# Halved weight splits, an earlier row eviction and moved logits and transposes in a fused attention and expert kernel

## The chip, the cores and the metric

The kernel runs on one core of one Trainium2 chip. A core has a matrix engine (TensorE, PE in the profile, with its weight loads as PEld), a vector engine (VectorE, DVE), a scalar engine (ScalarE, ACT), a general engine (GpSimd, POOL) and a queue engine that starts transfers (SyncE, SP). SBUF is the memory on the core, PSUM the memory with eight banks that TensorE writes its results to. The metric is the device time of one execution in microseconds (us).

## The reference

The input is an attention with a decaying state over 4 batches, 8 heads, 768 positions and a head dimension of 48, followed by a layer of 8 experts of which each token uses one:

```python
# attention, for each position t
cur = einsum('bhd,bhe->bhde', u * k_t, v_t)
y[t] = einsum('bhd,bhde->bhe', r_t, state + cur)
state = w_t[..., None] * state + einsum('bhd,bhe->bhde', k_t, v_t)
# experts, x is y as 3072 tokens x 384
logits = x @ w_gate + modality_bias[modality_id]
e = argmax(logits); gate = softmax(logits)[e]
out = gate * (relu(x @ w1[e]) @ w2[e])        # 384 -> 1024 -> 384
```

## The kernel before

**Attention.** The 3072 tokens are cut into NU = 24 units of 128, six for each batch. A loop runs i from -2 to 23 and calls `att_iter(i)`, which works on several units at once: the scans of unit a = i + 2, the products of unit m = i + 1, and the result of unit z = i. For unit a, VectorE makes two scans over the decays w (B, L251, and E, L254, 128x516 each). After that, R = r times E (L215) and, later, K = k times B (L221). POOL makes G = r times k behind the E scan (L256) and dV = v times dT (L262). For unit m, TensorE transposes K into bank pK (L283, not for the last unit of a batch), multiplies K with R into the banks pS0 and pS1 (L301), VectorE masks these into A (L303), and KT times v goes to pU (L310), from which ACT makes the next state SP. TensorE also sums G into a few columns of bank pT (`delta`, L233), which ACT copies to dT (L235). For unit z, TensorE adds a part from the state (L331) and a part from A (L337) into bank pY.

**What follows a unit's result.** One step later `x_rows` (L361) has VectorE evict pY plus dV into the rows of x, named xp. One more step later `x_cols` (L368) has TensorE transpose these rows into pT, ACT copies them to xT (L369), and `logits` (L374) multiplies xT with the gate's weights into bank pR. When 12 units are done, `route_a`, `route_b` (in `hook_b`) and `table` choose the experts on VectorE and make tables of blocks. They are put into the steps 14, 15 and 16 as hooks. From then on POOL scatters the rows of x to memory by expert, 2 or 3 units a step.

**Weights.** Products with weights are made of three: each weight is split into a rounded part wh (a cast on ACT, L206) and a rest wl (a subtraction, L207), and x and h likewise. Before the experts are known, w1 and w2 of a first expert e0 are loaded to raw[0] and raw[1] in quarters in steps 7 to 14 (L687). `w_split(0, f, 1, POOL)` splits one of the eight 128x384 parts f of w1 at a time, in the steps that `SPLITS = (10, 11, 12, 13, 14, 14, 16, 22)` names. In steps 3 to 6 the hooks `setup_a` to `setup_d` make a table of biases. They use a corner of raw[0] (bt2) for its second half.

**Experts.** Then come blocks of 256 tokens of one expert, for which `seq` gives the order. For block q, `blk_t` transposes the tokens into the banks pK and pU, ACT casts them to xh and VectorE subtracts to xo. `blk_up` makes the 1024 inner columns in four groups g of 18 matmuls each (L596), in the banks pS0, pS1 and pT in turn. ACT (hh, L601) and VectorE (hl, L602) empty each group. `blk_down` (L613) accumulates into pY and pX. In block 0 the last two units' transposes stand behind its groups 0 and 1, in pT, and their logits behind groups 2 and 3. The splits for the next block go along (`w_split(1, g)` on POOL and `w_split(0, g)` on VectorE).

**Order.** Every engine works in the order in which the program is written, and waits where data or a bank isn't ready. Tiles of one tag (`pt`) share a PSUM bank: pT holds the sums of `delta`, the transposes of `x_cols`, and a third of the groups of `blk_up`.

Of the kernel before, what the change touches and what calls it, by code (L numbers as in the profile page):

```python
# [9 lines left out]
F32 = mybir.dt.float32  # L10
# [4 lines left out]
ALU = mybir.AluOpType  # L15
# [37 lines left out]
def kernel(ctx: ExitStack, tc: tile.TileContext, rkw, vt, wf, cst, mid, wg, bias, w1, w2, out):  # L53
# [103 lines left out]
    m1 = cp.tile([P, 2, NU], F32, name="m1")  # L157
    bt2 = raw[0][:, 0, 0:NU * E].rearrange("p (a e) -> p a e", a=NU)
    bv = bb.rearrange("p (a e) -> p a e", a=2)
# [43 lines left out]

    def w_split(k, q, n=2, eng=None):
        sl = slice(n * q, n * q + n)
        nc.scalar.copy(out=wh[k][:, sl], in_=raw[k][:, sl])  # L206
        (eng or (nc.vector, nc.gpsimd)[k]).tensor_tensor(out=wl[k][:, sl], in0=raw[k][:, sl], in1=wh[k][:, sl].bitcast(F32), op=ALU.subtract)  # L207

# [14 lines left out]
    def first(n):  # L223
        return n % NCH == 0

    def ok(n):
        return 0 <= n < NU
# [9 lines left out]
    hooks = []  # L237
    done = iter(range(FC))

    SPLITS = (10, 11, 12, 13, 14, 14, 16, 22)  # L240

    def att_iter(i):
# [17 lines left out]
        if ok(z):  # L260
            dV = wt(z, "dV", [P, H, D], 2)
            nc.gpsimd.tensor_tensor(out=dV, in0=T["v", z].rearrange("p (a b) -> p a b", a=H),  # L262
                                    in1=T["dT", z].rearrange("p a b -> p (a b)")[:, :, None].to_broadcast([P, H, D]), op=ALU.mult)
        for _ in range(SPLITS.count(i)):
            w_split(0, next(done), 1, nc.gpsimd)
        if ok(z - 1):
            x_rows(z - 1)
# [6 lines left out]
        if ok(m):  # L274
# [5 lines left out]
            if not last:  # L280
# [6 lines left out]
                nc.scalar.copy(out=KT, in_=pK)  # L287
            if ok(z - 2):
                x_cols(z - 2, pT)
# [8 lines left out]
            for p in range(4):  # L298
                for hh in range(2):
                    q = slice(64 * hh, 64 * hh + 64)  # L300
                    nc.tensor.matmul(out=pS[hh][:, p], lhsT=K[q, p], rhs=R[q, p], start=True, stop=True)  # L301
            for hh in range(2):
                nc.vector.tensor_tensor(out=A[:, hh], in0=pS[hh], in1=mask[:, None, :].to_broadcast([P, 4, P]), op=ALU.mult)  # L303
            if ok(a):
                mk_k(a)
            if not last:
# [10 lines left out]
                for hh in range(2):  # L317
                    q = slice(64 * hh, 64 * hh + 64)
                    nc.scalar.copy(out=SPb[a % 3][q, :, hh], in_=SP[q])
        elif ok(z - 2):  # L320
            x_cols(z - 2, pt(m, "pT"))
        if ok(z - 2):
            logits(z - 2)
        if hooks:
            hooks.pop(0)()
        if ok(z):
            A, R, v, pY = T["A", z], T["R", z], T["v", z], pt(z, "pY")
            if not first(z):
                for p in range(4):
                    for q in (0, 64):  # L330
                        nc.tensor.matmul(out=pY[q:q + 64, 2 * p * D:2 * (p + 1) * D], lhsT=R[:, p, q:q + 64],  # L331
                                         rhs=SPb[z % 3][:, p].rearrange("p a b -> p (a b)"),
                                         start=(p == 0), stop=False, skip_group_check=True)
            for h in range(H):
                p, hh = divmod(h, 2)
                for q in (0, 64):
                    nc.tensor.matmul(out=pY[q:q + 64, h * D:(h + 1) * D], lhsT=A[:, hh, p, q:q + 64], rhs=v[:, h * D:(h + 1) * D],  # L337
                                     start=(first(z) and h == 0), stop=True, skip_group_check=True)
        if ok(m):
            delta(m)  # L340
# [235 lines left out]
    def blk_t(q):  # L576
# [10 lines left out]
        X["x", q] = (xh, xo)  # L587

    def blk_up(q, g):
        xh, xo = X["x", q]  # L590
        pp = pt(f"u{q}_{g}", ("pS0", "pS1", "pT")[(q * (FC // 2) + g) % 3] if isinstance(q, int) else f"pS{g % 2}", (P, 2, BT))
        for i in range(2):
# [90 lines left out]
    for i in range(-2, NU):  # L683
# [10 lines left out]
        if i == NU - 1:  # L694
            prep.close()
        att_iter(i)
        if i >= -1 and ok(i + 3):
            loadv(i + 3)
# [263 lines left out]
```

## Time and profile before

| what | us |
|---|---|
| median of 3 runs | 396.58 |
| the runs | 396.58, 398.23, 391.73 |
| the profiled execution | 392.17 |
| its span in the trace | 390.3 |
| first matmul of block 0, from the span's start | 154.5 |
| mean granted TensorE clock | 0.965 |

The trace is of one execution. In its views a row of the timeline gives the start, the duration, the engine, the line, the operation, output and inputs, and in brackets how long the engine was idle before it and what ended that. A duration in a timeline includes the latency of the instruction, so on one engine the next one can start a little before the end of the one before. Pieces of the chain of waits give start and length. A row of busy times by stretch gives start and end, the length, busy time and count for PE, PEld, DVE, ACT and POOL, then the granted clock as a share of full, the share of the DMA engines and their GB/s.

### The profile page before, as it was taken

The numbers are of one execution on the slowest core, as the hardware profiler recorded it, in microseconds if no ns is written. First come the engines' busy times: TensorE is split into PE (matmuls) and PEld (weight loads), VectorE is DVE, ScalarE is ACT, GpSimd is POOL, SyncE is SP. The second block draws the span as 40 slices with busy tenths as digits, with TensorE's granted clock in tenths as the row PEclk, the third lists the DMA queues.
The fourth block names the chain that finished last, engine by engine and source line by source line (L and its number), as shares of the span: only waits on it lengthen the run. The fifth ranks groups of instructions, "written<-read, shape, count | busy, mean of one in ns | idle before, by whom it ended". The sixth has DMA issues, their size and how long they took to land.

```text
span 390.3 us, 10893 instructions
## 1 busy us (share of the span) xinstructions
PE 360.5 (92%) x4280; PEld 343.7 (88%) x4280; DVE 246.7 (63%) x407; ACT 234.1 (60%) x480; POOL 226.3 (58%) x194
## 2 busy tenths in 40 slices
PE   5899899998877999999999999999999999999990
PEld 2688888887866988899999999999999999999990
DVE  6899999999998992675265936344261716651010
ACT  2476466668544662667468586777777675854330
POOL 6234643544878742576688895747466474736440
PEclk9589999999996999999999999999999999999996
DMA  7975779999467851001126543131313474166000
GB/s 153 216 159 135 169 187 215 226 235 211 110 162 193 210 187 51 1 3 42 60 103 223 154 171 117 48 122 39 104 43 101 127 260 135 45 208 196 9 28 21
DMA packets 18464, 50.52 MB, mean 129 GB/s; under 512 B 2917, under 2 KB 10635, under 8 KB 18404
## 3 DMA queue, kind: packets, MB, share of 16 engines
q1 hardware_dynamic: 15268, 40.28, 40.5%
q0 software_dynamic: 3136, 9.47, 6.8%
q8 instruction: 35, 0.57, 0.7%
q14 instruction: 25, 0.20, 0.2%
HBM read 72.89 MB, written 11.63 MB: 217 GB/s over the span
## 4 chain that ended last, share of the span: by engine, by line
PE 64%; DVE 18%; issue 10%; ACT 2%; POOL 2%; DMA 2%; SPq 0%; POOLq 0%; DVEq 0%; ACTq 0%
PE pS_u L596 18%; PE pY_d L613 13%; PE pX_d L613 13%; PE pT_u L596 9%; DVE B L251 5%; DVE A L303 4%; DVE K L221 3%; DVE R L215 3%; PE pS L301 3%; DMA in<-rkw 2%; PE pK_x L584 1%; PE pY L337 1%; PE pK L283 1%; PE pY L331 1%; PE pT L368 1%
## 5 line engine op out<-in xcount | busy, mean ns | idle before, releaser
L207 POOL TENSOR_TENSOR wl<-raw,wh 128x768 fp32r<-128x768 f32 (+1 forms) x60 | 104.1, 1743 | 72.9 <-ACT wh L206 72.8
L206 ACT CAST wh<-raw 128x768 fp32r<-128x768 f32 (+1 forms) x104 | 83.4, 805 | 35.1 <-PE pX_d L613 24.9
L256 POOL TENSOR_TENSOR G<-in 128x512 f32<-128x512 f32 x24 | 31.3, 1303 | 58.4 <-PE pS L301 30.6
L602 DVE SCALAR_TENSOR_TENSOR hl<-pS_u,hh 128x512 fp32r<-128x512 f32 x32 | 22.1, 690 | 55.7 <-ACT hh L601 55.7
L211 ACT COPY pX<-in 128x512 f32<-128x512 f32 x47 | 27.7, 590 | 48.1 <-DVE R L215 39.6
L596 PE MATMUL pS_u<-xh,wh 128*128 128x256 f32 x192 | 54.6, 284 | 0.0
L596 PE MATMUL pS_u<-xo,wh 128*128 128x256 f32 x192 | 54.1, 282 | 0.0
L596 PE MATMUL pS_u<-xh,wl 128*128 128x256 f32 x192 | 54.1, 282 | 0.0
L207 DVE TENSOR_TENSOR wl<-raw,wh 128x768 fp32r<-128x768 f32 x44 | 49.4, 1122 | 2.8 <-ACT wh L206 1.8
L621 POOL DMA_INDIRECT out<-ot,xl x25 | 32.5, 1301 | 10.9 <-ACT ot L620 5.3
L596 PEld LDWEIGHTS pS_u<-xo,wh 128*128 128x128 f32 x192 | 36.2, 189 | 0.0
L596 PEld LDWEIGHTS pS_u<-xh,wl 128*128 128x128 f32 x192 | 36.2, 189 | 0.0
L601 ACT ACTIVATE hh<-pS_u 128x512 fp32r<-128x512 f32 x32 | 19.2, 599 | 28.3 <-PE pS_u L596 28.3
L596 PEld LDWEIGHTS pS_u<-xh,wh 128*128 128x128 f32 x192 | 36.0, 188 | 0.1
L602 DVE SCALAR_TENSOR_TENSOR hl<-pT_u,hh 128x512 fp32r<-128x512 f32 x16 | 11.0, 689 | 39.1 <-ACT hh L601 39.1
L613 PE MATMUL pY_d<-wh,hh 128*128 128x384 f32 x96 | 33.5, 349 | 0.0
L303 DVE TENSOR_TENSOR A<-pS,cs 128x512 f32<-128x512 f32 x48 | 30.7, 681 | 4.0 <-PE pS L301 3.9
L251 DVE TENSOR_TENSOR_SCAN B<-in,d1b 128x516 f32<-128x516 f32 x24 | 30.9, 1288 | 3.5 <-DMA in<-rkw 3.5
L613 PE MATMUL pX_d<-wh,hh 128*128 128x384 f32 x96 | 32.5, 338 | 0.0
L613 PE MATMUL pX_d<-wl,hh 128*128 128x384 f32 x96 | 32.4, 338 | 0.0
L613 PE MATMUL pY_d<-wl,hh 128*128 128x384 f32 x96 | 32.4, 338 | 0.0
L613 PE MATMUL pY_d<-wh,hl 128*128 128x384 f32 x96 | 32.4, 338 | 0.0
(187 smaller groups left out, 910.8 us busy)
## 6 DMA issues: line engine op xcount, KB each, us to landing
raw<-w SPq DMA_DIRECT2D x52, 768.0 KB
in<-rkw SPq DMA_DIRECT2D x46, 288.9 KB
xl<-xs SPq DMA_DIRECT2D x12, 386.0 KB
v<-vt SPq DMA_DIRECT2D x24, 192.0 KB
wg<-wf SPq DMA_DIRECT2D x8, 576.0 KB
raw<-w SPq DMA_DIRECT2D x8, 384.0 KB
xs<-zt SPq DMA_DIRECT2D x8, 193.0 KB
out<-ot,xl POOLq DMA_INDIRECT x25, 3.6
```

The costliest lines, as they stand in the source:

```text
L206: nc.scalar.copy(out=wh[k][:, sl], in_=raw[k][:, sl])
L207: (eng or (nc.vector, nc.gpsimd)[k]).tensor_tensor(out=wl[k][:, sl], in0=raw[k][:, sl], in1=wh[k][:, sl].bitcast(F32), op=ALU.subtract)
L211: nc.scalar.copy(out=pt(a, "pX", (P, 4, P)), in_=src.rearrange("p (a b) -> p a b", a=4))
L215: nc.vector.tensor_tensor(out=R, in0=T["pX", a], in1=T["E", a].rearrange("p (a b) -> p a b", a=4)[:, :, 0:P], op=ALU.mult)
L251: nc.vector.tensor_tensor_scan(out=Bt[:, 516:0:-1], data0=w[:, 516:0:-1], data1=d1b[:, 516:0:-1], initial=0.0, op0=ALU.mult, op1=ALU.max)
L256: ins_g = nc.gpsimd.tensor_tensor(out=G, in0=r, in1=k, op=ALU.mult)
L303: nc.vector.tensor_tensor(out=A[:, hh], in0=pS[hh], in1=mask[:, None, :].to_broadcast([P, 4, P]), op=ALU.mult)
L596: nc.tensor.matmul(out=pp[:, i], lhsT=wsrc[0][:, f, c * P:(c + 1) * P], rhs=xsrc[:, c], start=(n == 0), stop=(n == 3 * KC - 1))
L601: nc.scalar.activation(out=hh, in_=pp, func=AF.Relu)
L602: nc.vector.scalar_tensor_tensor(out=hl, in0=pp, scalar=0.0, in1=hh.bitcast(F32), op0=ALU.max, op1=ALU.subtract)
L613: nc.tensor.matmul(out=X["y", q][j], lhsT=hsrc[:, i, j * P:(j + 1) * P], rhs=wsrc[1][:, f], start=(f == 0 and n == 0), stop=(f == FC - 1 a ...
L621: ins = nc.gpsimd.indirect_dma_start(out=out[:, :], out_offset=bass.IndirectOffsetOnAxis(ap=xl[:, j, DM + 1:DM + 2].bitcast(I32), axis=0), ...
```

## The change

It has five parts.

1. The second half of the table of biases, bt2, lies in the last part of raw[1] and no longer in the first of raw[0].
2. w1's first split is made in 16 halves of 128x192 by a new function. Steps 9 to 13 have one half each, step 14 four, steps 16 and 22 two each. Three halves are left, which are made behind step 23.
3. `x_rows(16)` stands at the end of step 16 and no longer behind the scans of step 17.
4. In step 22 the transposes of unit 20 stand behind the products into pS, its logits stand between the two parts of pY, and the transposes of unit 21 stand behind those, in bank pK. The logits of unit 21 stand at the end of step 23.
5. In block 0 the four groups of `blk_up` use pS0 and pS1 in turn and leave pT to the transposes.

```diff
-    bt2 = raw[0][:, 0, 0:NU * E].rearrange("p (a e) -> p a e", a=NU)
+    bt2 = raw[1][:, FC - 1, 0:NU * E].rearrange("p (a e) -> p a e", a=NU)
...
+    def w_split_half(n):
+        f, c = n // 2, n % 2 * (DM // 2)
+        part = lambda t: t[:, f, c:c + DM // 2]
+        nc.scalar.copy(out=part(wh[0]), in_=part(raw[0]))
+        nc.gpsimd.tensor_tensor(out=part(wl[0]), in0=part(raw[0]), in1=part(wh[0]).bitcast(F32), op=ALU.subtract)
...
-    done = iter(range(FC))
+    done = iter(range(2 * FC))
...
-    SPLITS = (10, 11, 12, 13, 14, 14, 16, 22)
+    SPLITS = {9: 1, 10: 1, 11: 1, 12: 1, 13: 1, 14: 4, 16: 2, 22: 2}
...
-        for _ in range(SPLITS.count(i)):
-            w_split(0, next(done), 1, nc.gpsimd)
-        if ok(z - 1):
+        for _ in range(SPLITS.get(i, 0)):
+            w_split_half(next(done))
+        if ok(z - 1) and i != NJ + 5:
             x_rows(z - 1)
...
-            if ok(z - 2):
+            if ok(z - 2) and i < NU - 2:
                 x_cols(z - 2, pT)
...
+            if i == NU - 2:
+                x_cols(z - 2, pT)
...
-        elif ok(z - 2):
-            x_cols(z - 2, pt(m, "pT"))
-        if ok(z - 2):
+        if ok(z - 2) and i < NU - 2:
             logits(z - 2)
...
+            if i == NU - 2:
+
+                logits(z - 2)
+                x_cols(z - 1, pt(m + 1, "pK"))
...
+        if i == NU - 1:
+            logits(z - 2)
+        if i == NJ + 4:
+
+            x_rows(z)
...
+    UPB = ("pS0", "pS1", "pT")
...
-        pp = pt(f"u{q}_{g}", ("pS0", "pS1", "pT")[(q * (FC // 2) + g) % 3] if isinstance(q, int) else f"pS{g % 2}", (P, 2, BT))
+        pp = pt(f"u{q}_{g}", UPB[(q * (FC // 2) + g) % 3] if isinstance(q, int) and q else f"pS{g % 2}", (P, 2, BT))
...
+        if i == NU - 1:
+            for n in done:
+                w_split_half(n)
```

**Order on POOL, steps 9 to 11.** G and dV are the two products of a step, wl is the subtraction of the split. Before:

```order
L256 TENSOR_TENSOR G_1184<-in_87 128x512
L262 TENSOR_TENSOR dV_1186<-v_949,dT_1170 128x384
L256 TENSOR_TENSOR G_1291<-in_85 128x512
L262 TENSOR_TENSOR dV_1293<-v_1065,dT_1277 128x384
L207 TENSOR_TENSOR wl_69<-raw_66,wh_68 128x384
L256 TENSOR_TENSOR G_1377<-in_86 128x512
L262 TENSOR_TENSOR dV_1379<-v_1172,dT_1363 128x384
L207 TENSOR_TENSOR wl_69<-raw_66,wh_68 128x384
```

After, the same steps:

```order
L262 TENSOR_TENSOR G_1184<-in_87 128x512
L268 TENSOR_TENSOR dV_1186<-v_949,dT_1170 128x384
L213 TENSOR_TENSOR wl_69<-raw_66,wh_68 128x192
L262 TENSOR_TENSOR G_1293<-in_85 128x512
L268 TENSOR_TENSOR dV_1295<-v_1065,dT_1279 128x384
L213 TENSOR_TENSOR wl_69<-raw_66,wh_68 128x192
L262 TENSOR_TENSOR G_1379<-in_86 128x512
L268 TENSOR_TENSOR dV_1381<-v_1172,dT_1365 128x384
L213 TENSOR_TENSOR wl_69<-raw_66,wh_68 128x192
```

The first half goes into step 9, which had no part of the split, and each part has half the columns.

**Order on VectorE, from the end of the tables in step 16 to R in step 17.** Before:

```order
L494 SCALAR_TENSOR_TENSOR tab<-pR_x,tabe 128x4
L251 SCALAR_TENSOR_TENSOR B_2057<-in_86,d1b 128x516
L253 RECIPROCAL d1e<-B_2057 128x4
L254 SCALAR_TENSOR_TENSOR E_2058<-in_86,d1e 128x516
L361 TENSOR_TENSOR xp_1592<-pY_2009,dV_1953 128x384
L215 TENSOR_TENSOR R_2069<-pX_2059,E_2058 128x512
```

After:

```order
L509 SCALAR_TENSOR_TENSOR tab<-pR_x,tabe 128x4
L376 TENSOR_TENSOR xp_1594<-pY_2017,dV_1959 128x384
L257 SCALAR_TENSOR_TENSOR B_2066<-in_86,d1b 128x516
L259 RECIPROCAL d1e<-B_2066 128x4
L260 SCALAR_TENSOR_TENSOR E_2067<-in_86,d1e 128x516
L221 TENSOR_TENSOR R_2077<-pX_2068,E_2067 128x512
```

The eviction of unit 16, xp, has moved from behind the scans to ahead of them.

**Order on TensorE, from step 22 to the last product of step 23.** pT and pK written from xp are transposes of x, pR_x are logits, pK_x and pU_x the transposes of block 0. Before:

```order
L368 MATMUL pT_2676<-cs,xp_1592 128x128 x3
L301 MATMUL pS_23_2683<-R_2580,K_2612 128x128
...
L374 MATMUL pR_x<-cs,xT_2677 64x8 x6
L331 MATMUL pY_2701<-SPb_128,R_2421 64x96 x8
L337 MATMUL pY_2701<-v_2402,A_2599 64x48 x16
L233 MATMUL pT_2676<-cs,G_2575 64x2 x8
L584 MATMUL pK_x_0_2742<-cs,xl_2513 128x128 x4
L584 MATMUL pU_x_2_2749<-cs,xl_2513 128x128 x2
L368 MATMUL pT_2754<-cs,xp_1592 128x128 x3
L374 MATMUL pR_x<-cs,xT_2755 64x8 x6
L331 MATMUL pY_2766<-SPb_129,R_2580 64x96 x8
L337 MATMUL pY_2766<-v_2511,A_2682 64x48 x16
```

After:

```order
L307 MATMUL pS_23_2688<-R_2588,K_2620 128x128
...
L383 MATMUL pT_2686<-cs,xp_1594 128x128 x3
L337 MATMUL pY_2705<-SPb_128,R_2429 64x96 x8
L389 MATMUL pR_x<-cs,xT_2698 64x8 x6
L383 MATMUL pK_2720<-cs,xp_1594 128x128 x3
L347 MATMUL pY_2705<-v_2410,A_2607 64x48 x16
L239 MATMUL pT_2686<-cs,G_2583 64x2 x8
L599 MATMUL pK_x_0_2758<-cs,xl_2521 128x128 x4
L599 MATMUL pU_x_2_2765<-cs,xl_2521 128x128 x2
L337 MATMUL pY_2770<-SPb_129,R_2588 64x96 x8
L347 MATMUL pY_2770<-v_2519,A_2687 64x48 x16
L389 MATMUL pR_x<-cs,xT_2721 64x8 x6
```

The products into pS stand first, the transposes of unit 21 have moved ahead of block 0's transposes and into bank pK, and its logits have moved behind the last pY.

More of the change, by code (lines that the diff above doesn't have):

```diff
@@ L202, in w_raw, with w_split @@
                           in_=(w1, w2)[k][ds(e, 1), :, part * n * DM:(part + 1) * n * DM].rearrange("a p c -> (a p) c"), **kw)
-    def w_split(k, q, n=2, eng=None):
+    def w_split(k, q, n=2):
         sl = slice(n * q, n * q + n)
         nc.scalar.copy(out=wh[k][:, sl], in_=raw[k][:, sl])
-        (eng or (nc.vector, nc.gpsimd)[k]).tensor_tensor(out=wl[k][:, sl], in0=raw[k][:, sl], in1=wh[k][:, sl].bitcast(F32), op=ALU.subtract)
+        (nc.vector, nc.gpsimd)[k].tensor_tensor(out=wl[k][:, sl], in0=raw[k][:, sl], in1=wh[k][:, sl].bitcast(F32), op=ALU.subtract)
+    def w_split_half(n):
[3 more added lines that the diff above has]
+        nc.gpsimd.tensor_tensor(out=part(wl[0]), in0=part(raw[0]), in1=part(wh[0]).bitcast(F32), op=ALU.subtract)
     def rk_psum(a, src):
```

## The prediction

> **What bounds the kernel now.** I read the page first (span, clock, chain), then busy time by stage, then the timelines of single engines around each edited place, and last the chain of waits through the end of the attention stage.
>
> ```profile
> span 390.3 us, 10893 instructions
> PE 360.5 (92%) x4280; PEld 343.7 (88%) x4280; DVE 246.7 (63%) x407; ACT 234.1 (60%) x480; POOL 226.3 (58%) x194
> PEclk9589999999996999999999999999999999999996
> ...
> 60.67:94.66 33.99, 31.03 (x670) 27.95 (x666) 33.55 (x50) 22.16 (x64) 15.78 (x16) 1.00 0.97 222
> ...
> 116.66:129.29 12.63, 10.01 (x169) 9.20 (x165) 10.87 (x18) 5.60 (x17) 10.26 (x11) 0.73 0.74 196
> ...
> 145.68:154.53 8.85, 7.54 (x173) 6.86 (x169) 3.41 (x7) 3.02 (x9) 2.62 (x3) 1.00 0.27 81
> ...
> 175.38:361.00 185.62, 185.62 (x1342) 185.45 (x1341) 91.60 (x156) 127.00 (x199) 120.74 (x81) 1.00 0.37 121
> ```
>
> The stage rows give the stretch, its length, then the busy time of PE, PEld, DVE, ACT and POOL, the granted clock and the DMA share. From 60.67 to 94.66 VectorE is busy 33.55 of 33.99: it sets the pace of the attention steps. From 116.66 on, the granted clock is only 0.73 and both engines have gaps. From 145.68 to 154.53 VectorE is busy 3.41 of 8.85 and TensorE sets the end. From 175.38 on, TensorE is busy without a gap for 185.62 us, so what a part before it gains is handed on to the end. Step i below is the call att_iter(i); unit n is its chunk of 128 tokens.
>
> **The split in halves.** In steps 10 to 13 POOL subtracts one 128x384 part of w1 behind dV, and the next step's first scan starts while it runs:
>
> ```profile
> L251 DVE TENSOR_TENSOR_SCAN B<-in,d1b x24: 1169/1224/1617, 6.0 to 140.2; 128x516 f32<-128x516 f32 x24
> ...
> 77.17 1.62 DVE L251 TENSOR_TENSOR_SCAN B<-in,d1b 128x516 f32<-128x516 f32 x1
> ...
> 94.66 1.60 DVE L251 TENSOR_TENSOR_SCAN B<-in,d1b 128x516 f32<-128x516 f32 x1
> ...
> 70.28 0.84 POOL L262 TENSOR_TENSOR dV<-v,dT 128x384 f32<-128x384 f32 x1
> ...
> 76.69 1.01 POOL L207 TENSOR_TENSOR wl<-raw,wh 128x384 fp32r<-128x384 f32 x1
> ...
> 158.77 1.82 POOL L207 TENSOR_TENSOR wl<-raw,wh 128x768 fp32r<-128x768 f32 x1 [7.07 <-ACT wh L206]
> ```
>
> The median scan takes 1.224 us (the first row: minimum, median, maximum in ns). The four that start at 77.17 to 94.66 take about 1.6, some 0.39 longer. POOL's subtraction ends at 76.69 + 1.01 = 77.70, so it overlaps the scan by 0.53, and 0.39 of that is lost. A 128x192 subtraction isn't in the trace. From 1.01 and 1.82 for twice the columns (0.81 per 384) I estimate 0.60 us. It would end at 77.29 and overlap by 0.12, which costs 0.09. Four scans save 4 x 0.30 = **1.2 us**. The ends are 4 x 0.39 = 1.56 if nothing collides, and 0 if a collision costs a fixed amount. The new half in step 9 starts where dV ends, at 70.28 + 0.84 = 71.12, and ends at about the 71.71 where the untouched next scan starts: 0. The parts of steps 14, 16 and 22 stay as large, and each extra instruction adds about 0.2 us (2 x 0.60 against 1.01) on POOL, which waits there. The casts on ACT shrink and hide in the same way. Three halves are left for the time behind step 23. POOL (busy 2.62 of 8.85 there) does them in 1.8 us before block 0's last group reads them some 8 us later.
>
> **The place of the table of biases.** w1's first quarter no longer waits for the sum that reads the table; it moves up in the DMA queue, and so do the two loads behind it. Nothing in step 7 waits for these: 0.
>
> **Rows ahead of the scans in step 17.** The eviction of unit 16 (xp) goes ahead of the scan:
>
> ```profile
> 116.66 1.23 DVE L251 TENSOR_TENSOR_SCAN B<-in,d1b 128x516 f32<-128x516 f32 x1
> ...
> 119.28 0.53 DVE L361 TENSOR_TENSOR xp<-pY,dV 128x384 f32<-128x384 f32 x1
> ...
> 121.52 0.68 DVE L221 TENSOR_TENSOR K<-pX,B 128x512 f32<-128x512 f32 x1
> ...
> 127.49 1.29 DVE L303 TENSOR_TENSOR A<-pS,cs 128x512 f32<-128x512 f32 x2 [1.62 <-PE pS L301]
> ...
> 119.87 0.88 PE L331 MATMUL pY<-SPb,R 128*64 128x96 f32 x16 [2.46 <-DVE xp L361]
> ...
> 120.00:121.00 1.00, 1.00 (x28) 1.00 (x30) 1.00 (x3) 0.55 (x2) 1.00 (x2) 0.87 0.57 201
> ...
> 125.45 2.06 PE pS L301 x16
> ...
> 124.42 1.18 POOL L555 DMA_INDIRECT xs<-xp,posT  x1 [0.31 <-issue]
> 125.62 1.28 POOL L256 TENSOR_TENSOR G<-in 128x512 f32<-128x512 f32 x1
> 126.85 0.84 POOL L262 TENSOR_TENSOR dV<-v,dT 128x384 f32<-128x384 f32 x1
> ```
>
> For VectorE the move is neutral up to R: 0.45 earlier work, 0.45 later scans. TensorE waits 2.46 us for xp. Right behind it, in the bin from 120 to 121, its clock falls below full (0.87), and the mean of 0.73 over the 12.63 us of this stage amounts to 2 x 0.27 x 12.63 = 6.8 us at half speed. pS takes 2.06 there, and VectorE waits 1.62 us for it. Now xp ends near 117.2, and pY starts at once instead of at 119.87. But the next thing in TensorE's order is pK, which needs the K that ends at 122.2, so its gap doesn't go: it moves behind pY and delta (some 2.3 us of work) to about 119.55 to 122.2, **2.65 us long**. At full clock pS is then done before R and the whole 1.62 is gained. POOL is what comes next: it has no idle time before G at 125.62 (124.42 + 1.18), since three scatters, G and dV fill a step. G waits for the E scan, now 0.45 later, so POOL's work comes 0.45 later while VectorE comes 1.6 earlier. dV then ends near 128.15, under a scan that starts near 127.6, and again one step later: 0.57 and 0.7 of overlap, at 0.39 lost per 0.53, make 0.9. I take 1.62 - 0.9 = **0.7 us**. The ends are 1.62 without the collisions, and -2: if the clock halves inside the new gap, the next step's pS is late as well, about as much again as the 1.62 seen.
>
> The Trainium skill, TensorE: Matmul & The Clock Gate, in Part 1 and in "HAM oscillation — how this bites in real kernels", counts activity in free-running windows of about 3.4 us and advises "no PE-idle gaps >~3.4µs". By that rule the new gap of 2.65 would leave the clock up, and so should the old one of 2.46 have done. Here the clock fell right behind that shorter gap, so the rule doesn't excuse the new gap.
>
> **Logits and transposes at the end.** The pieces of the chain of waits carry start and length:
>
> ```profile
> 145.08 0.68 DVE L221 TENSOR_TENSOR K<-pX,B 128x512 f32<-128x512 f32 x1
> ...
> 146.39 0.55 PE pT L368 x3
> 146.93 1.09 PE pS L301 x16
> 148.02 0.45 PE pR_x L374 x12
> 148.47 0.71 PE pY L331 x16
> 149.19 0.92 PE pY L337 x32
> 150.10 0.43 PE pT L233 x16
> 150.53 0.60 PE pK_x L584 x4
> ...
> 152.97 0.71 PE pY L331 x16
> 153.68 0.92 PE pY L337 x32
> 154.60 2.35 PE pS_u L596 x18
> 156.95 0.33 PE pT_('x', 0)_2848 L368 x3
> 157.28 2.16 PE pS_u L596 x18
> ...
> 159.96 0.48 ACT xT L369
> ...
> 160.48 2.42 PE pT_u L596 x18
> ...
> 161.33 0.68 DVE L602 SCALAR_TENSOR_TENSOR hl<-pS_u,hh 128x512 fp32r<-128x512 f32 x1
> ...
> 166.74 0.22 PE pU_x L584 x2
> ```
>
> Before, the transposes of unit 20 waited for dT and held pS. Now pS(23) starts when K is there, at 145.08 + 0.68 and its signal, 145.85, and ends at 146.94. Then, each at its length above and its transposes at some 0.4: x_cols(20) to 147.4, pY's first part 148.1, logits(20) 148.55, x_cols(21) 148.95, pY's second part 149.9, delta 150.3, blk_t(0) (0.60 + 0.22) 151.15, pY(23) 152.8, logits(21) 153.23. The first matmul of block 0 starts there and not at 154.60: **1.37 us**. Its cover is that xT(21) is copied while pY runs, where logits(21) used to wait for it. xo must be there by 153.2, and by the same shift is at 152.6. The low end is 0.5, if only pS's wait goes; the high end is 1.9, if nothing queues.
>
> **Two banks for block 0.** The third group waited for the copy of xT, since it shared bank pT with the transposes: 157.28 + 2.16 + 0.33 = 159.77, and it started at 160.48. Now it uses pS0, whose hl is read long before: **0.7 us**. What is late next is the fourth group, which now needs bank pS1, free at 161.33 + 0.68 = 162.01, which is 2.57 behind the second group's end at 159.44. It starts 0.33 + 2.16 + 0.45 = 2.94 behind. A margin of 0.37 is left; the ends are 0 and 0.7.
>
> **Sum.** 1.2 + 0.7 + 1.37 + 0.7 = 4.0 us off the profiled execution, whose own time is 392.17 (1.87 around the span): 388.2. The median of the three runs, 396.58, stands 4.4 above that execution, and the runs go from 391.73 to 398.23. Nothing in one trace says which of these the new kernel will draw, so I set the sum against the mean of all four times shown, 394.7: **390.7 us**.
>
> **Rivals.**
> - *The half clock stays long.* It ends on the other side. The page's clock line starts with 9, 5 and 8 in slices of 9.8 us: some 13 us at half speed. If the gap of 2.65 brings that on, work such as pS takes 2.06 for the 1.09 of full clock, 1.89 times as long, and a step that fills TensorE to 31.03 of 33.99 takes 1.73 times as long. 13 us of it lose 13 x (1 - 1/1.73) = 5.5. Against 3.3 from the other terms that is 2.2 slower than before, 396.9. It decides from 7.8 us of half clock on (7.8 x 0.42 = 3.3). Against it: the old gap brought 6.8 us, in part covered.
> - *The clock stays up and POOL doesn't collide.* Then the largest values hold, 1.56 + 1.62 + 1.37 + 0.7 = 5.3, and the time is 389.4. For it: POOL's scatters may be over sooner, and the clock is full from 129 to the end of the stage. Against it are the drop behind 2.46 and POOL's full queue. The rule on gaps of the Trainium skill, TensorE: Matmul & The Clock Gate ("HAM oscillation"), excludes a drop of the clock here and so goes with this rival.
> - *The split and the bank change do nothing.* A half still collides in full because dV itself ends later, and the fourth group waits as the third did. Only 0.7 + 1.37 remain: 392.6. Against it: a margin of 0.37, and 0.41 less overlap per scan.
>
> **Chances.** The forecast 0.55, long half clock 0.10, all at their best 0.15, two parts without effect 0.20. The range runs from the lowest run less the best sum, 391.73 - 5.3 = 386.4, rounded to 386, up to the highest less the two remaining terms, 398.23 - 2.1 = 396.1, rounded to 396. A measurement of this kernel tells little under 2%. Faster by over 2% means under 388.6 against the median: reached by the sum if the new runs fall near the profiled execution and not near the median, and in the best case, 0.33 in all. Slower by over 2%, above 404.5, needs the long half clock twice: 0.02. The rest, 0.65, is within 2%.
>
> **What would show it.** Scans behind the splits at 1.2 to 1.35 us and not 1.6. TensorE's pY of unit 17 at once behind the tables, a gap of 2.5 to 2.7 us behind it, A of unit 19 without 1.6 us of waiting, then scans of 1.6 to 1.8 us in one or two steps beside dV. 1.2 to 1.5 us less from K of unit 23 to block 0's first matmul, no wait at its third group and none at its fourth. The forecast is wrong if the clock falls somewhere new, if the fourth group waits, or if the 185 us of gapless TensorE show new gaps.

## The result, and the profile after

| | median, us | runs, us | profiled execution, us | its span, us |
|---|---|---|---|---|
| before | 396.35 | 391.60 to 401.59 (20 runs) | 392.17 | 390.3 |
| after | 389.67 | 388.08 to 394.58 (20 runs) | 390.73 | 388.9 |

The ratio is 0.9881, with a 95% interval of 0.9842 to 0.992. On 396.35 that is 4.7 us less, between 3.2 and 6.3. Ten of the 20 runs after lie between 388.08 and 388.61, the others between 390.73 and 394.58, so no run lies at the median itself. All ratios here leave out runs more than 1.5% above the fastest of their kernel, so they can differ from the quotient of the medians.

First the page of the kernel after: span, busy times, and TensorE's clock in 40 slices of 9.7 us.

```profile
span 388.9 us, 10908 instructions
PE 361.0 (93%) x4280; PEld 344.3 (89%) x4280; DVE 248.2 (64%) x407; ACT 234.2 (60%) x488; POOL 230.0 (59%) x202
PEclk9599689999999999999999999999999999999996
```

Before, the clock line had a 6 in the 13th slice, which is full now. In its place stand a 6 and an 8 in the fifth and sixth, where the change moved no instruction. Busy times by stretch of the kernel after (PE, PEld, DVE, ACT, POOL, then the granted clock) show the stage of the scatters and the end of the attention:

```profile
116.00:130.00 14.00, 11.10 (x218) 9.59 (x218) 13.55 (x28) 7.24 (x23) 11.35 (x12) 1.00 0.75 201
145.85:154.18 8.33, 8.29 (x193) 7.55 (x188) 4.02 (x8) 4.52 (x15) 3.85 (x7) 1.00 0.27 89
```

In the first VectorE is busy for 13.55 of 14.00 us at a clock of 1.00, where the stretch of before had 0.73. In the second TensorE has no gap left (8.29 of 8.33). VectorE's timeline after, with the group of the first scan ahead of it (minimum, median and maximum in ns):

```profile
L257 DVE TENSOR_TENSOR_SCAN B<-in,d1b x24: 1168/1224/2490, 5.8 to 141.0; 128x516 f32<-128x516 f32 x24
...
79.64 1.22 DVE L257 TENSOR_TENSOR_SCAN B<-in,d1b 128x516 f32<-128x516 f32 x1
...
96.02 1.22 DVE L257 TENSOR_TENSOR_SCAN B<-in,d1b 128x516 f32<-128x516 f32 x1
...
117.65 0.55 DVE L376 TENSOR_TENSOR xp<-pY,dV 128x384 f32<-128x384 f32 x1
...
126.99 1.28 DVE L311 TENSOR_TENSOR A<-pS,cs 128x512 f32<-128x512 f32 x2
...
134.26 2.49 DVE L257 TENSOR_TENSOR_SCAN B<-in,d1b 128x516 f32<-128x516 f32 x1
```

The scans behind the splits, of which the first and the last stand here, take 1.22 us; they took about 1.6. The eviction of unit 16 stands ahead of the scans, and A of unit 19, at 126.99, waits for nothing. But one scan, of step 20, now takes 2.49. POOL's timeline after shows what lies under these scans:

```profile
79.15 0.59 POOL L213 TENSOR_TENSOR wl<-raw,wh 128x192 fp32r<-128x192 f32 x1
...
133.57 1.29 POOL L262 TENSOR_TENSOR G<-in 128x512 f32<-128x512 f32 x1
134.82 0.83 POOL L268 TENSOR_TENSOR dV<-v,dT 128x384 f32<-128x384 f32 x1
135.81 1.75 POOL L570 DMA_INDIRECT xs<-xp,posT  x1 [0.17 <-issue]
```

A half takes 0.59 us and ends at 79.74, 0.10 behind the scan's start: the scan loses nothing. G and dV run without a gap to 135.65, and the long scan ends at 136.75, 1.10 later. In the trace of before the split ended at 77.70 and the scan at 78.79, 1.09 later. So a scan that meets such a product or subtraction of POOL makes its whole pass behind it; of its usual 1.22 us only some 0.12 can lie under POOL. A scatter under way costs it nothing: the scan at 118.11 takes 1.22 although POOL's scatter runs from 117.65 to 118.62. The Trainium skill, SBUF — State Buffer, section "SBUF: two separate sides", says that VectorE (in an instruction with two inputs in SBUF, for one) and GpSimd have one pair of ports in common, held "for the whole instruction" by whichever starts first, while the other blocks. These rows agree with it. They show more than it says in one point: dV, begun at 134.82, went ahead of a scan that had already waited since 134.26.

The pieces of the chain of waits after, from pS of unit 23 on (start and length):

```profile
146.68 1.16 PE pS L307 x16
147.84 0.48 PE pT L383 x3
...
154.25 2.35 PE pS_u L614 x18
156.60 0.33 PE pT_('x', 0)_2864 L383 x3
156.93 2.16 PE pS_u L614 x18
159.09 0.33 PE pT_('x', 1)_2897 L383 x3
159.42 2.16 PE pS_u L614 x18
161.57 0.45 PE pR_x L389 x12
...
162.03 2.42 PE pS_u L614 x18
...
165.70 0.53 PE pY_d L631 x3
```

From K of unit 23 (145.85 in the trace after) to block 0's first matmul the chain takes 154.25 - 145.85 = 8.40 us, before 154.60 - 145.08 = 9.52. From there to the first matmul of `blk_down` it takes 165.70 - 154.25 = 11.45, before 166.96 - 154.60 = 12.36. (The table below takes the same points from the timeline, where these first matmuls start 0.07 and some 0.24 earlier.) Neither the third group nor the fourth waits. But the fourth needs bank pS1, which VectorE frees late, as its timeline after shows:

```profile
161.30 0.68 DVE L620 SCALAR_TENSOR_TENSOR hl<-pS_u,hh 128x512 fp32r<-128x512 f32 x1
```

That ends at 161.98, and the fourth group starts at 162.03.

So three parts gained what they were meant to, some 3.5 us, and the spans differ by only 1.4. The rest was lost early. TensorE, the clock by stretch (PE's busy time comes first, the clock stands behind POOL's) and VectorE of the kernel after, in steps 3 to 5:

```profile
39.65 0.55 PE L383 MATMUL pT<-cs,xp 128*128 128x128 f32 x3 [1.09 <-ACT dT L241]
```
```profile
38.00:39.00 1.00, 0.55 (x22) 0.47 (x16) 0.97 (x4) 0.94 (x4) 0.23 (x2) 1.00 0.08 16
39.00:40.00 1.00, 0.35 (x3) 0.31 (x3) 0.97 (x2) 1.00 (x6) 0.90 (x1) 1.00 0.65 175
...
41.00:42.00 1.00, 1.00 (x19) 0.85 (x15) 1.00 (x3) 0.00 (x0) 0.41 (x1) 0.70 1.12 234
42.00:46.00 4.00, 4.00 (x65) 3.95 (x65) 3.93 (x8) 0.70 (x2) 3.59 (x6) 0.50 0.21 43
```
```profile
49.82 1.29 DVE L311 TENSOR_TENSOR A<-pS,cs 128x512 f32<-128x512 f32 x2 [1.75 <-PE pS L307]
```

TensorE is busy 0.90 of the 2 us from 38 to 40, with one gap of 1.09. One to two microseconds later the clock halves, stays so to about 51.6 (the mean from 50 to 52 is 0.59), and VectorE waits 1.75 us and, one step later, 0.61 for pS. It is the same kind of loss as before's at step 17, at another place. The only edit near it is the place of the table of biases (part 1), and e1 and e4, which lack that edit, show a shorter fall there too (in e1 the clock is 0.58 and 0.50 from 42 to 44). Nor does the gap alone explain it, since TensorE's timeline of the kernel before has the same one:

```profile
39.60 0.55 PE L368 MATMUL pT<-cs,xp 128*128 128x128 f32 x3 [1.10 <-ACT dT L235]
```

There TensorE is busy 0.91 of the 2 us from 38 to 40, and the clock stays at 1.00 behind it. What decides is not shown.

### The profile page after: what moved, and what is told of

Read it like the earlier page. It is cut to its first block, busy times and chain, and to the rows that moved or that the text cites. A ratio compares the mean times of both kernels' runs of the same rounds, so it can differ in the third digit from the quotient of the medians.

```text
span 388.9 us, 10908 instructions
## 1 busy us (share of the span) xinstructions
PE 361.0 (93%) x4280; PEld 344.3 (89%) x4280; DVE 248.2 (64%) x407; ACT 234.2 (60%) x488; POOL 230.0 (59%) x202
## 4 chain that ended last, share of the span: by engine, by line
PE 63%; DVE 19%; issue 10%; POOL 2%; DMA 2%; ACT 1%; SPq 0%; POOLq 0%; DVEq 0%; ACTq 0%
PE pS_u L614 18%; PE pY_d L631 13%; PE pX_d L631 13%; PE pT_u L614 8%; DVE B L257 6%; DVE A L311 4%; DVE K L227 3%; DVE R L221 3%; PE pS L307 2%; DMA in<-rkw 2%; PE pK_x L599 1%; PE pY L347 1%; PE pY L337 1%; DVE d1e L259 1%; PE pK L289 1%
## 5 line engine op out<-in xcount | busy, mean ns | idle before, releaser
L207 POOL TENSOR_TENSOR wl<-raw,wh 128x768 fp32r<-128x768 f32 x52 | 96.9, 1872 | 67.3 <-ACT wh L206 67.3
L206 ACT CAST wh<-raw 128x768 fp32r<-128x768 f32 x96 | 79.3, 831 | 33.8 <-PE pX_d L631 24.2
L614 PE MATMUL pS_u<-xh,wh 128*128 128x256 f32 x198 | 56.4, 285 | 0.0
L614 PE MATMUL pS_u<-xo,wh 128*128 128x256 f32 x198 | 55.8, 282 | 0.0
L614 PE MATMUL pS_u<-xh,wl 128*128 128x256 f32 x198 | 55.8, 282 | 0.0
L207 DVE TENSOR_TENSOR wl<-raw,wh 128x768 fp32r<-128x768 f32 x44 | 51.1, 1160 | 3.1 <-ACT wh L206 2.2
L614 PEld LDWEIGHTS pS_u<-xo,wh 128*128 128x128 f32 x198 | 37.4, 189 | 0.0
L614 PEld LDWEIGHTS pS_u<-xh,wl 128*128 128x128 f32 x198 | 37.3, 189 | 0.0
L614 PEld LDWEIGHTS pS_u<-xh,wh 128*128 128x128 f32 x198 | 37.2, 188 | 0.1
```

Source lines behind the costliest of these rows:

```text
L207: (nc.vector, nc.gpsimd)[k].tensor_tensor(out=wl[k][:, sl], in0=raw[k][:, sl], in1=wh[k][:, sl].bitcast(F32), op=ALU.subtract)
L614: nc.tensor.matmul(out=pp[:, i], lhsT=wsrc[0][:, f, c * P:(c + 1) * P], rhs=xsrc[:, c], start=(n == 0), stop=(n == 3 * KC - 1))
```

## The experiments

The table gives the stages of each profiled execution in us: between the starts of the first scans (B) of steps 10, 15, 17 and 21, from K of unit 23 to block 0's first matmul, and from there to the first matmul of `blk_down`.

| kernel | 10 to 15 | 15 to 17 | 17 to 21 | K(23) to block 0 | up of block 0 | span |
|---|---|---|---|---|---|---|
| before | 30.74 | 14.21 | 23.56 | 9.45 | 12.18 | 390.3 |
| after | 29.25 | 14.68 | 22.87 | 8.33 | 11.28 | 388.9 |
| e1_halves | 29.26 | 14.22 | 22.94 | 9.99 | 12.34 | 388.9 |
| e2_rows | 30.73 | 14.68 | 26.36 | 10.05 | 12.18 | 393.6 |
| e3_end | 30.72 | 14.22 | 28.11 | 9.01 | 12.21 | 394.3 |
| e4_bank | 30.74 | 14.21 | 28.40 | 9.89 | 11.21 | 394.1 |
| e5_rows_back | 29.27 | 14.20 | 23.15 | 8.33 | 11.28 | 386.4 |
| e6_warm | 29.25 | 14.69 | 22.86 | 8.33 | 11.28 | 386.3 |
| e7_scat2 | 29.25 | 14.68 | 21.59 | 8.33 | 11.28 | 385.7 |
| e8_before_warm | 30.75 | 14.21 | 23.13 | 9.45 | 12.19 | 389.6 |
| e9_after_again | 29.26 | 14.68 | 26.39 | 9.02 | 11.29 | 391.2 |
| e10_rows_back_again | 29.27 | 14.21 | 28.48 | 8.86 | 11.30 | 392.0 |
| e11_warm_scat2 | 29.26 | 14.69 | 22.78 | 9.17 | 11.27 | 388.9 |
| e12_back_warm_scat2 | 29.26 | 14.21 | 24.88 | 9.17 | 11.27 | 388.8 |

e1 to e4 and e9 to e12 ran on one chip, on which the kernel before had medians of 397.23 and 396.99; e5 to e8 ran on another, on which it had 391.96 (390.86 to 398.01).

**One part of the change at a time.** The theory: each part has its own gain at its own place. The rival: some do nothing, or only bring a half clock somewhere. Each kernel is the one before with one part.

e1_halves, the split in halves with its new steps, the table of biases left where it was:

```diff
-    SPLITS = (10, 11, 12, 13, 14, 14, 16, 22)
+    SPLITS = {9: 1, 10: 1, 11: 1, 12: 1, 13: 1, 14: 4, 16: 2, 22: 2}
...
-            w_split(0, next(done), 1, nc.gpsimd)
+            w_split_half(next(done))
```

> The kernel before with the split of w1 in halves alone. Theory (each part pays its own term): the four scans behind the parts of steps 10 to 13 take 1.22 us and not 1.6, so from the scan of step 10 to the scan of step 15 it is 29.25 us instead of 30.74, and the time falls by about 1.5 us. Rival (the split in halves frees nothing by itself, what POOL gets back is lost behind it): the scans are short, but from step 10 to block 0's first matmul it is as long as before, and the time stays within 0.5 us.

Stage 10 to 15 falls from 30.74 to 29.26, as in the kernel after: 1.48 us, and the place of bt2 plays no part in it. In the trace of e1 the longest first scan of all 24 is 1.34, in that of before 1.62:

```profile
L257 DVE TENSOR_TENSOR_SCAN B<-in,d1b x24: 1169/1224/1339, 6.1 to 138.3; 128x516 f32<-128x516 f32 x24
```

Yet the median of 12 runs is 395.79 and the ratio 0.9997 (0.9962 to 1.0033). A gain of 0.4% that is plain in the trace drowns in runs from 390.81 to 397.55.

e2_rows, the eviction of unit 16 at the end of step 16:

```diff
-        if ok(z - 1):
+        if ok(z - 1) and i != NJ + 5:
             x_rows(z - 1)
...
+        if i == NJ + 4:
+            x_rows(z)
```

> The kernel before with the eviction of unit 16 ahead of the scans of step 17 alone. Theory: VectorE no longer waits 1.6 us for pS in step 18, but one of the scans of steps 19 and 20 runs into POOL's G and dV and takes 2 us or more, so from the scan of step 17 to the scan of step 21 only 0 to 0.7 us are gained. Rival (the move only saves where TensorE's clock falls behind the old gap): the scans stay at 1.22 us and the gain is the whole 1.6 us in a run whose clock falls in the kernel before, and 0 in others; the median time falls by 1 us or more with a smaller spread.

395.72, ratio 0.9952 (0.9907 to 0.9998). TensorE starts pY early, but the clock falls all the same, from 119 on. pS of that step takes 1.99 in the trace of e2, as it took 2.06 before:

```profile
124.35 1.99 PE L301 MATMUL pS<-R,K 64*128 64x128 f32 x16
```

Moving the gap doesn't keep the clock up. The ratio lies just under 1, though no stage of the trace gains; e5, e10 and e12 below test the same part with the rest of the change in place.

e3_end, the new places of logits and transposes in steps 22 and 23:

```diff
+            if i == NU - 2:
+                logits(z - 2)
+                x_cols(z - 1, pt(m + 1, "pK"))
...
+        if i == NU - 1:
+            logits(z - 2)
```

> The kernel before with the moved logits and transposes of steps 22 and 23 alone. Theory: from K of unit 23 to block 0's first matmul it is 8.35 us instead of 9.45, and the time falls by 1.1 us. Block 0's third group still waits about 0.7 us for the copy of xT. Rival (the gain is lost at the third group, which waits for ACT anyway): the first matmul is earlier, but from K of unit 23 to the first matmul of blk_down it is as long as before, 21.8 us.

K(23) to block 0 takes 9.01. On this chip e1, e2 and e4, whose order is the old one there, take 9.99, 10.05 and 9.89, so the part is worth 0.9 to 1.0 here. The median is 396.09, ratio 0.9955 (0.9901 to 1.0009). Its profiled execution lost more at steps 17 to 21, in code that is untouched, since the clock was at half for 17 us (busy times by stretch of e3):

```profile
121.00:125.00 4.00, 3.03 (x45) 2.61 (x41) 3.93 (x7) 1.79 (x9) 3.23 (x4) 0.50 0.49 151
125.00:138.00 13.00, 13.00 (x138) 11.55 (x138) 7.25 (x12) 5.90 (x15) 9.66 (x9) 0.50 0.72 180
```

e4_bank, two banks for block 0:

```diff
-        pp = pt(f"u{q}_{g}", ("pS0", "pS1", "pT")[(q * (FC // 2) + g) % 3] if isinstance(q, int) else f"pS{g % 2}", (P, 2, BT))
+        pp = pt(f"u{q}_{g}", ("pS0", "pS1", "pT")[(q * (FC // 2) + g) % 3] if isinstance(q, int) and q else f"pS{g % 2}", (P, 2, BT))
```

> The kernel before with two banks for block 0 alone. Theory: the third group starts right behind the transposes, the fourth doesn't wait, and from block 0's first matmul to the first of blk_down it is 11.5 us instead of 12.2; the time falls by 0.7 us, too little for the runs to tell. Rival (the fourth group takes over the wait): 12.2 us as before, with a wait ahead of the fourth group.

The groups of block 0 take 11.21 and not 12.18: 0.97 us, with no wait at the fourth group. The median is 396.34, ratio 1.0015 (0.9977 to 1.0052). Three parts are thus shown at their places, and none by the medians.

**Is the early eviction worth anything, and what does the clock do?** The theory now: the eviction is worth nothing, and the wait that it seemed to remove belongs to the half clock. The rival: it is worth its 0.7.

e5_rows_back, the kernel after without the early eviction:

```diff
-        if ok(z - 1) and i != NJ + 5:
+        if ok(z - 1):
             x_rows(z - 1)
...
-        if i == NJ + 4:
-            x_rows(z)
```

> The changed kernel with the eviction of unit 16 back behind the scans of step 17. Theory (the early eviction pays little in executions with a full clock, since POOL's collision eats it): the fastest runs lie within 0.5 us of those of the changed kernel, 388.1 to 388.6, and more of the runs lie 1.5 to 4 us above them. Rival (the move is worth the whole wait): the fastest runs too are 1.6 us slower.

388.37, ratio 0.991 (0.9878 to 0.9942). Nine of the 12 runs lie between 387.32 and 389.1, as the theory said of the fastest. But only three lie higher, not more than the ten of 20 of the kernel after, which were not taken beside it.

e6_warm, the kernel after with products of zeros as filler in TensorE's gaps (NJ is 12, so the last are in step 17). They write to bank pK when it is free; nothing reads them:

```diff
+    def warmk(n):
+        wp = pt("wk", "pK")
+        for i in range(n):
+            nc.tensor.matmul(out=wp, lhsT=wm[:, 0:P], rhs=wm, start=(i == 0), stop=(i == n - 1))
...
+            if i in (4, 10, 16):
+                warmk(4)
...
+        if i == NJ + 5:
+            warmk(10)
```

> The changed kernel with 10 more matmuls of zeros (bf16, 128x512, into bank pK) on TensorE behind delta of step 17, and 4 each ahead of the transposes of steps 4, 10 and 16, where TensorE waits. Theory (the spread between runs is a halved clock that falls behind such gaps): the granted clock is 1.00 from 25 us to 360 us in the profile, nearly all runs lie at 388 to 389, and the median falls by 1 to 2 us against the changed kernel's 389.67. Rival (the spread comes from something else, such as loads): the runs spread over 388 to 394 as before.

388.2, ratio 0.9898 (0.9859 to 0.9938). From step 15 to 21, e5 without the early eviction takes 14.20 + 23.15 = 37.35, and e6 with it 14.69 + 22.86 = 37.55. The eviction costs 0.2. In both traces a scan of step 20 meets G and dV (e5's, then e6's):

```profile
131.58 2.50 DVE L257 TENSOR_TENSOR_SCAN B<-in,d1b 128x516 f32<-128x516 f32 x1
```
```profile
131.57 2.49 DVE L262 TENSOR_TENSOR_SCAN B<-in,d1b 128x516 f32<-128x516 f32 x1
```

So the collision that the prediction charged to the move comes without it too. With the filler the clock is full from 22 us to the end, on the page of e6 and in its stretch:

```profile
PEclk9599999999999999999999999999999999999996
...
22.00:116.00 94.00, 88.03 (x1854) 78.51 (x1855) 92.24 (x159) 59.68 (x177) 50.77 (x60) 1.00 0.80 186
```

Six runs lie within 1.1 us, 387.84 to 388.95, where e5 without the filler spread from 387.32 to 402.04. The filler takes away the dear runs and doesn't lower the best (e6 has 6 runs, e5 has 12).

e8_before_warm, the filler in the kernel before (in step 17 ahead of pY, where its gap is):

```diff
+            if i in (4, 10, 16):
+                warmk(4)
...
+        if i == NJ + 5:
+            warmk(9)
```

> The kernel before with 9 more matmuls of zeros on TensorE ahead of pY in step 17, where it waits 2.46 us for the eviction, and 4 each in steps 4, 10 and 16. Theory (its runs at 395 to 398 are those in which the clock halves behind these gaps): nearly all runs lie near 391.6 to 392.5, and the median falls by 3 us or more. Rival: the runs spread as before around 396.

391.53, ratio 0.9991 (0.9969 to 1.0013). Its 12 runs lie between 391.3 and 392.17, while the kernel before had up to 398.01 on the same chip. The median didn't fall by the 3 us expected: on this chip that of the kernel before is 391.96, and only two of its 23 runs lie above 393.2. With filler on both sides the whole change is e8 against e6: 391.53 - 388.2 = **3.33 us**, and the runs don't overlap. (In the trace of e8 the clock falls once, for some 3 us near 91, which lengthens no stage.) The stages say the same: 1.49 - 0.2 + 1.12 + 0.90 = 3.31. VectorE's and POOL's timelines of e8 show the collision in the old order too, once the clock is full in these steps:

```profile
132.84 2.50 DVE L256 TENSOR_TENSOR_SCAN B<-in,d1b 128x516 f32<-128x516 f32 x1
```
```profile
133.41 0.82 POOL L267 TENSOR_TENSOR dV<-v,dT 128x384 f32<-128x384 f32 x1
```

The scan ends at 135.34, 1.11 behind dV's end at 134.23. Not every execution has it: in e1, with the old order and a full clock from 114 on, A waits 0.43 and 0.45 us for TensorE, and all scans of these steps take 1.22 to 1.25.

**Can the collision be avoided?** The theory: three scatters a step fill POOL, so that G and dV slip under the scan; two leave room. e7_scat2 is the kernel after with two scatters in each step:

```diff
-        drain(2 if i == NJ + 3 else 3)
+        drain(2)
```

> The changed kernel with two scatters of rows per step in steps 15 to 20 instead of two, three, three, three and one. Theory (POOL's lag behind three scatters a step puts G and dV under the scan of step 20): no scan above 1.4 us in steps 17 to 21, from the scan of step 17 to that of step 21 it is 21.6 us instead of 22.9, and the fastest runs are 1.2 us faster, near 387. Rival (the later scatters hold up block 0's rows): the transposes of block 0 wait for their load, and nothing is gained.

387.44 (386.54 to 390.23), ratio 0.9898 (0.9849 to 0.9947). Stage 17 to 21 falls to 21.59, 1.27 less than in e6, which is the price of one blocked scan (2.49 - 1.22). VectorE, POOL and TensorE in the trace of e7:

```profile
132.21 1.22 DVE L257 TENSOR_TENSOR_SCAN B<-in,d1b 128x516 f32<-128x516 f32 x1
```
```profile
130.94 0.83 POOL L268 TENSOR_TENSOR dV<-v,dT 128x384 f32<-128x384 f32 x1
...
135.14 1.28 POOL L262 TENSOR_TENSOR G<-in 128x512 f32<-128x512 f32 x1 [0.93 <-PE pS L307]
```
```profile
121.52 0.63 PE L289 MATMUL pK<-cs,K 128*128 128x128 f32 x4 [2.15 <-DVE K L227]
```

dV is done 0.44 us ahead of the scan, and POOL now waits itself. Two of the six runs still lie at 390.1 and 390.23. TensorE's row shows the moved gap as forecast, 2.15 us behind pY and delta, here without a fall of the clock behind it.

**The same on the other chip.** e9_after_again is the kernel after itself, without an edit:

> The changed kernel once more, for a comparison on the same chip with the next three. Theory (its runs above 388.6 are those in which TensorE's clock halves behind a gap): runs in groups, the lowest near 388.2, others 2 to 4 us and more above.

392.69 (388.82 to 394.99), ratio 0.9916 (0.9852 to 0.998). That is 3.3 us of 396.99, near the sum of the stages, though the interval reaches from 0.8 to 5.9. In its profiled execution 3.5 us more than in after went at steps 17 to 21, where the clock is also at half for some 7 us from 118 on. ACT's and TensorE's timelines of e9:

```profile
131.47 0.17 ACT L241 COPY dT<-pT 128x8 f32<-128x8 f32 x1 [3.55 <-remote]
```
```profile
131.69 0.56 PE L383 MATMUL pT<-cs,xp 128*128 128x128 f32 x3 [3.13 <-ACT dT L241]
```

ACT sits idle for 3.55 us ahead of a small copy, ended by what the trace calls remote, and TensorE waits behind it. e2 and e4 have such a wait in one of these steps too, of 3.51 and 3.66.

e10_rows_back_again, the edit of e5 again:

> The changed kernel with the eviction of unit 16 back behind the scans of step 17, beside the changed kernel. Theory (at full clock the early eviction is worth nothing; its worth is that the clock falls less often or for a shorter time): the lowest runs equal those of the changed kernel within 0.5 us, and the median is 1 us or more above it, if the clock falls on this chip at all. Rival (the early eviction doesn't matter for the clock either, since the gap on TensorE only moves): the medians are within 1 us of each other.

392.22 (388.0 to 395.35), ratio 0.9878 (0.9803 to 0.9953). The theory's 1 us or more isn't there. Beside e9 the early eviction again shows no difference, 0.5 us with intervals that overlap almost wholly.

e11_warm_scat2 has the edits of e6 and e7 together:

```diff
+        if i == NJ + 5:
+            warmk(10)
...
-        drain(2 if i == NJ + 3 else 3)
+        drain(2)
```

> The changed kernel with the matmuls of zeros in its gaps (10 behind delta of step 17, 4 each in steps 4, 10 and 16) and with two scatters per step. Theory: both gains add, no scan above 1.4 us and no clock below full in the attention steps; nearly all runs at 386.5 to 387.6, and faster than the changed kernel by 1.2 us in its best runs and by more in the median. Rival (the filled gap and the moved scatters get in each other's way): no better than the changed kernel.

390.7, ratio 0.9882 (0.9834 to 0.993), all six runs within 389.69 to 390.87. The filler steadies the time on this chip too: e9 spread over 6.2 us, e11 over 1.2. But the expected 386.5 to 387.6 is missed: the median is 2.0 below that of e9, while the lowest run is 0.9 above its lowest. The clock is full to the end, and the scan of step 20 takes 1.23, but stage 17 to 21 (22.78) doesn't fall as in e7. ACT's timeline of e11 has the wait again:

```profile
134.68 0.17 ACT L246 COPY dT<-pT 128x8 f32<-128x8 f32 x1 [2.16 <-remote]
```

So that wait isn't caused by the clock.

e12_back_warm_scat2 goes without the early eviction, with the filler ahead of pY and two scatters:

```diff
-        if i == NJ + 4:
-            x_rows(z)
...
+        if i == NJ + 5:
+            warmk(9)
...
+        drain(2)
```

> The same with the eviction of unit 16 back behind the scans, and 9 matmuls of zeros ahead of pY in step 17 in place of the 10 behind delta. Theory (the early eviction costs 0.2 us where the clock is full): 0 to 0.3 us faster than with the early eviction. Rival (the early eviction is worth its wait once POOL's collision is gone): 1 us or more slower than with it.

391.6 (390.66 to 393.0), ratio 0.9911 (0.9861 to 0.9961). Expected were 0 to 0.3 us less than in e11; the median is 0.9 more. The clock's mean was 0.79 between 122 and 130, in spite of the filler, while e11's was full, so the pair doesn't price the eviction at a full clock. What it is worth where the clock falls stays open: the runs of e2 and e12 speak for it, those of e10 don't.

The fastest of all is e7, 387.44. On its chip stand beside it 388.2 for the kernel after with filler and 388.37 for it without the early eviction; the kernel after as it is was not run on that chip, and e11 shows no certain gain from two scatters on the other.

## Why the prediction was right, and where its terms were off

**The time.** Forecast 390.7, measured 389.67. The sum of 4.0 lies inside the 3.2 to 6.3 us of the ratio's interval, and so does the 3.33 of e8 against e6. The best half of the runs came where the sum from the profiled execution put them, 388.2. That the median came out within 1 us of the forecast is in part luck. It lies between two groups of runs, the mean of four times (394.7) stood 1.7 below the median of the 20 runs before, and the sum is 2.7 short of the difference of the medians, so two errors nearly cancel. Within the sum, too, the eviction's missing gain is made up for in part by the other three terms, which came to 3.51 and not 3.27. The change doesn't settle the clock either. That the medians differ by 6.7 and not by 3.3 is no shown effect of it; the interval takes in 3.3.

**The split in halves** (forecast 1.2, measured 1.49). The mechanism was right, and a half takes 0.59 as estimated (0.60). Mis-sized was the remainder, "overlap by 0.12, which costs 0.09": it costs nothing (the halves overlap by 0.08 to 0.11), because a blocked scan loses its overlap less some 0.12 and not a fixed share of it. That is nearly the upper end of 1.56.

**The place of the table of biases** (forecast 0). Stage 10 to 15 is the same with it and without it (29.25, and 29.26 in e1).

**Rows ahead in step 17** (forecast 0.7 gained, measured 0.2 lost at full clock). This step failed, by a size within its two ends. It took the half clock behind the old gap, and with it the 1.62 us wait of A, as a consequence of the order. The wait is one of the half clock: in e8, the same order with a full clock, A has no wait, as its row in VectorE's timeline shows (no bracket behind it):

```profile
125.58 1.28 DVE L310 TENSOR_TENSOR A<-pS,cs 128x512 f32<-128x512 f32 x2
```

The half clock doesn't go with the order either. e5 has the old order without filler and a gap of 1.69 us ahead of pY, which starts at 118.41, but the clock is full from 114 on and A doesn't wait. In e2, with the eviction moved, the clock falls. The step also charged the collision to the move; e5 and e8 have it without the move. In the traces of before and after, the two stages fall from 14.21 + 23.56 to 14.68 + 22.87, by 0.2, and not by 0.7, since the clock that stayed up let POOL block the scan for 1.27. The forecast of a gap that only changes its place was right in kind, but its length in the profile after is less:

```profile
118.25 0.55 PE L337 MATMUL pY<-SPb,R 128*64 128x96 f32 x8
...
119.80 0.37 PE L337 MATMUL pY<-SPb,R 128*64 128x96 f32 x2 [0.35 <-issue]
...
123.55 0.63 PE L289 MATMUL pK<-cs,K 128*128 128x128 f32 x4 [1.28 <-DVE K L227]
```

In TensorE's timeline pY starts at once, is drawn out by idle stretches that the trace puts down to "issue", that is to nothing it shows, and leaves 1.28 and not 2.65; e7 has 2.15.

**Logits and transposes at the end** (forecast 1.37, measured 1.12). The order came out piece by piece as listed. Most lengths were low: x_cols takes 0.48 and not 0.4, pS 1.16 and not 1.09, pY's first part 0.81 and not 0.71, since the pieces were priced by those of the old order. The logits, at 0.30 and 0.32 and not 0.45, gave some of it back.

**Two banks** (forecast 0.7, measured 0.90). The wait of 0.71 went, the group behind it takes 2.16 where it took 2.42 after its wait, and the fourth group takes 2.42 and not 2.35. The fourth group's margin of 0.37 is there in e4 (0.35). In the kernel after only 0.05 of it is left, since VectorE is done with the second group, behind a weight split, 2.89 us after that group's end (161.98 against 159.09) and not 2.57.

**The sum, closed.** 1.49 + 0.22 + 1.12 + 0.90 = 3.73 less 2.47 lost at the half clock of steps 4 and 5 (the scan of step 10 starts at 74.18, before at 71.71), and 0.15 gained behind block 0's first part, which nothing here explains, make the 1.4 between the spans.

**Its signs.** One sign that the prediction names for being wrong came true: the clock fell somewhere new, at 41.4. That other kernels fall there too, and that half of the runs are 2.1 us or more faster than the profiled one, speak against the change as its cause, but no experiment settles it. The scans of 1.6 to 1.8 us beside dV became a single one of 2.49.

**The rivals.** The long half clock exists, with 17 us in e3, but nothing shows that the change brings it. "All at their best" failed on the collision. "Two parts without effect" was wrong about the two it named; a third was the one without effect. The Trainium skill, TensorE: Matmul & The Clock Gate ("HAM oscillation"), asks for "no PE-idle gaps >~3.4µs". The traces differ: the clock fell behind a gap of 1.09 with TensorE 45% busy over 2 us, stayed up behind the same gap in the kernel before, and stayed up behind one of 2.15 in e7.

## What to carry to other kernels

Price a part from a stretch in which nothing else is wrong: a wait that stands behind a half clock belongs to the clock, not to the order of the work. Filling a matrix engine's gaps with products of zeros is a cheap way to compare two versions when the clock scatters their times by more than they differ (here 0.9 to 2.3 us of spread with it, 3.7 to 14.7 without). It is no guarantee, since the clock still fell in e8 and e12. Where VectorE's scans read two operands from SBUF, keep GpSimd's products and subtractions from being under way when they start; the scans are not slowed but wait to the end of that work.

## What the runs showed of the hardware that was not expected

- The clock fell behind a gap of 1.09 us and then stayed at half for about 10 us (41.4 to 51.6) in the kernel after, and for 17 us in e3, but for only some 3 us, at no cost to a stage, near 111 in e5 and 112 in e7. The same gap left the clock up in the kernel before. Times differ between kernels whose code is the same there: stage 17 to 21 takes 23.56, 28.11 and 28.40 in before, e3 and e4 (e4 with a remote wait of 3.66 in it).
- GpSimd loses to VectorE likewise: a scatter issued under the long scan takes 1.75 us instead of about 0.98 and ends 0.81 behind the scan, in the kernel after (137.56 against 136.75) and in e8 (134.40 + 1.75 = 136.15, against 135.34).
- On one chip ACT waits 2.2 to 3.7 us, for what the trace calls remote, in one of the steps 18 to 20, in e2, e4, e9, e10 and e11, in e11 at a full clock. It isn't in the traces of e1, e3 and e12 of that chip, nor in those of e5 to e8. What it waits for stays open. On that chip the stretch from K(23) to block 0 is also 0.4 to 0.8 us longer than on the other, with either order.
